# Softmax sums of the first six pairs on TensorE, and second weight pieces in earlier steps

## The chip, the cores and the metric

The kernel runs on one core of a Trainium2 chip. The metric is the time of one execution in microseconds of device time. The engines of the core each work through a queue of their own, in order: TensorE (PE, matrix products), VectorE (DVE), ScalarE (ACT), GpSimd (POOL) and SyncE (SP, which here only issues DMAs). They wait for one another by semaphores.

## The reference

Attention with soft-capped scores, and behind it a channel-mix block (batch 8, 12 heads, 448 positions, head size 64, model width 768, inner width 1024), all in 32-bit floats:

```
scores = cap * tanh(q @ k.T / sqrt(64) / cap)
attn = exp(scores - max(scores))
attn = attn / (sum(attn) + 1e-9)
x = attn @ v                       # heads side by side: (8, 448, 768)
xk = mu_k * x + (1 - mu_k) * x_prev   # x_prev: x one position earlier
xr = mu_r * x + (1 - mu_r) * x_prev
out = sigmoid(xr @ w_r) * (relu(xk @ w_k) ** 2 @ w_v)
```

The weights come as 64-bit floats, which the kernel reads as pairs of 32-bit words and turns into 32-bit floats on the chip.

## The kernel before, in words

Two heads make a pair, and there are 48 pairs. A table of operations, `STEP`, is written out once per step i (0 to 54), and the order of its words is the order of each engine's queue. In one step the stages of different pairs stand side by side: scores, tanh, exp and the reductions of pair i; the value products and the reciprocals of pair i-1; normalizing and mixing of pair i-2; loading of pair i+3. No scheduler changes that order.

Scores are computed transposed, keys on the partitions and 448 queries along the row, in four groups S0 to S3 (three of 128 keys for both heads, one with the last 64 keys of both). Each group is three products, since q and k are split into a high and a low part (`qk_high`, `qk_low`, on POOL: names qkh and qkl). PSUM holds two groups at a time, so S2 waits for the first tanh of its step and S3 for the second, S0 of the next step for the third and S1 of the next step for the fourth. ACT runs tanh and exp on each group (names p). PE's order in a step is S0, S1, the value products V of the pair before (name pv; in even steps also the "tails", the products of the last 64 keys of two pairs), S2, and S3.

The softmax sum runs over keys, that is over partitions. Before, DVE adds within 32x32 blocks while it transposes them (`red`, line 240), four DMAs gather the partial sums into 32 partitions (`gather`), DVE adds these and forms the reciprocal (`recip`), one DMA stores it to DRAM and two load it back, spread over 64 partitions each (`rec_store`, `rec_load`). `norm` (line 265) multiplies the value product by it. Then ACT scales the shifted row (`mix_old`, between the third tanh and the third exp in ACT's queue), DVE adds the other part (`mix_new`, name xk, line 280) and POOL splits it into xkh and xkl.

From step 7 on PE also multiplies the mixed x by w_k in every step, in four portions of six products (`K`, name kps, two PSUM banks in `ps_k`), and ACT applies relu and stores the result.

Alongside, the weights are converted in 44 pieces of 384 columns. One piece is loaded in each step; `more` loads a second one in some steps, before in steps 6 to 10. At a step's end ACT takes the absolute value of a loaded piece; in the next step DVE runs five instructions on the first piece ("f", lines 412 to 420: wt, wa, wa, wt, wsq), which stand ahead of the reductions, and if there is a second piece, five more in `weight_rest`, behind the third reduction. POOL adds the two parts (`weight_sum`) and, for w_k, writes the high part wkh; DVE subtracts the low part at the start of the next step (`weight_low`, name wkl). In POOL's queue weight_sum stands ahead of qk_high and qk_low of the step, then come xkh and xkl, then weight_sum of a second piece.

After the 48 pairs comes a second stage with the products by w_v and w_r, which the change does not touch.

Of the kernel before, what the change touches and what calls it, by code (L numbers as in the profile page):

```python
# [10 lines left out]
F32 = mybir.dt.float32  # L11
F32R = mybir.dt.float32r
AF = mybir.ActivationFunctionType
ALU = mybir.AluOpType
# [3 lines left out]
B, H, S, D = 8, 12, 448, 64  # L18
# [11 lines left out]
P = 128  # L30
# [12 lines left out]
HALF = (slice(0, 64), slice(64, 128))  # L43
NB = 2 * S // 32
P1, P2, P3, P4, P5, P6, P7 = range(7)
LATE = 12


# [3 lines left out]

STEP = """gather load_v weight_load more weight_low S0 S1 V S2 f f f f f tanh0 exp0 red0
weight_sum tanh1 exp1 red1 norm recip rec_store K qk_high qk_low tanh2 relu mix_old k_store mix_new x_high x_low gate_old
K exp2 red2 weight_rest weight_sum relu k_store S3 K K tanh3 exp3 red3 gate_new relu k_store weight_abs load_qk rec_load tail_open x_store weight_store"""


def f(ap):
# [3 lines left out]
class Body:  # L62
# [61 lines left out]
    def init_sums(self, pool):  # L124


        nc = self.nc
        self.r1, self.sq, self.sr = [], [], []
        for j in range(2):
            self.r1.append(pool.tile([P, NB, 4], F32, name=f"r1_{j}"))  # L130
            nc.gpsimd.memset(self.r1[j], 0.0)
            for h in range(2):
                p = slice(64 - 64 * ((h + j) % 2), 96 - 64 * ((h + j) % 2))
                nc.vector.tensor_copy(self.r1[j][p, h * NB // 2:(h + 1) * NB // 2, 3], self.grd[p].to_broadcast([32, NB // 2]))
            self.sq.append(pool.tile([32, 4, NB, 4], F32, name=f"sq_{j}"))
            self.sr.append(pool.tile([32, 32], F32, name=f"sr_{j}"))
            nc.gpsimd.memset(self.sr[j], 1.0)

    def init_attn(self):
        self.raw, self.QK, self.rawv, self.S, self.P32, self.PV, self.R, self.rs = ({} for _ in range(8))  # L140
        self.tails = []


# [72 lines left out]
    def values(self, i):  # L216

        nc, v = self.nc, self.rawv.pop(i)
        self.PV[i] = pv = self.ps_v.tile([P, 512], F32, name="pv")
        for g in range(3):  # L220
            ph = self.P32.pop((i, g))
            for h, p in enumerate(HALF):
                nc.tensor.matmul(pv[p, 0:S], v[:, g, h, :], ph[:, h, :], start=(g == 0), stop=False)  # L223
        self.tails.append((i, v))
        if i % 2:

            for j, v in self.tails:
                ph = self.P32.pop((j, 3))
                for h, p in enumerate(HALF):
                    t = HALF[(h + j) % 2]  # L230
                    nc.tensor.matmul(self.PV[j][p, 0:S], v[t, 3, h, :], ph[t, 0, :], start=False, stop=True)  # L231
            self.tails = []

    def red(self, i, g):
        r1, p32 = self.r1[i % 2], self.P32[i, g]
        for p, h, out in [(slice(0, P), slice(0, 2), r1[:, :, g])] if g < 3 else \
                [(HALF[(h + i) % 2], slice(0, 1), r1[HALF[(h + i) % 2], h * NB // 2:(h + 1) * NB // 2, 3]) for h in range(2)]:
            self.nc.vector.tensor_reduce(out=out, in_=p32[p, h].rearrange("p h (b k) -> p (h b) k", k=32),  # L240
                                         axis=mybir.AxisListType.X, op=ALU.add, apply_transpose=True)

    def gather(self, i):
        for q in range(4):
            self.nc.sync.dma_start(self.sq[i % 2][:, q], self.r1[i % 2][32 * q:32 * q + 32])

    def recip(self, i):
        nc, t = self.nc, self.sr[i % 2]
        nc.vector.tensor_reduce(out=t[:, 0:NB], in_=self.sq[i % 2].rearrange("l q x g -> l x q g"),
                                axis=mybir.AxisListType.XY, op=ALU.add)  # L250
        nc.vector.reciprocal(t[:, 0:NB], t[:, 0:NB])
        self.rs[i] = self.up.tile([32, 32], F32, name="rs")
        nc.vector.transpose(out=self.rs[i], in_=t)

    def rec_store(self, i):
        self.nc.sync.dma_start(self.rec_d[i].rearrange("h (b k) -> (h b) k", k=32), self.rs.pop(i)[0:NB])

    def rec_load(self, i):
        r = self.up.tile([P, S], F32, name="r", bufs=1)
        for h in range(2):  # L260
            self.nc.sync.dma_start(r[HALF[h]], self.rec_d[i][h:h + 1, :].to_broadcast([64, S]))
        self.R[i] = r
# [374 lines left out]
    def step(self, i, KS):  # L637
# [2 lines left out]
        if self.maxima and i < NPAIR:  # L640
            self.row_maxima(i)
        pair = dict(load_qk=i + 3, qk_high=i + 2, qk_low=i + 2, load_v=i, S=i, tanh=i, exp=i, red=i)
        pair.update(dict.fromkeys("V gather recip rec_store rec_load".split(), i - 1))
        pair.update(dict.fromkeys("norm mix_old mix_new x_high x_low gate_old gate_new x_store".split(), i - 2))
        for op in STEP.split():
            j = pair.get(op)
# [10 lines left out]
            elif op == "tail_open":  # L657
                self.tail_open(i)
            elif op == "f":
                if i <= NPAIR:  # L660
                    self.fill()
            elif op == "more":
                if i in (6, 7, 8, 9, 10):
                    self.weight_load()
            else:
                getattr(self, op)()
# [170 lines left out]
```

## Time and profile before

| | us |
|---|---|
| median of 3 runs (951.23 to 955.11) | 951.86 |
| the profiled execution | 953.09 |
| its span, first to last instruction | 951.3 |
| PE busy | 898.3 |
| DVE busy | 749.8 |
| ACT busy | 633.3 |
| POOL busy | 400.0 |

The rows are read in microseconds from the span's start. A busy time is what an engine spent on its instructions; the bracket at a row's end is the idle time just ahead of it on that engine, with the instruction that ended it. Matmuls are pipelined: two that follow one another overlap in their rows, so a stretch of them is measured from the start of the first to the start of what comes next.

### The profile page before, as it was taken

The page shows a single profiled execution, that of the slowest core. Times are in us where ns is not written, and L with a number is a line of the kernel's source. Part 1 is how long each engine was busy: PE and PEld are TensorE (multiplying, and loading weights), DVE is VectorE, ACT ScalarE, POOL GpSimd, SP SyncE. Part 2 cuts the span into 40 slices and gives each one's busy share as a digit, 9 for nine tenths or more (in the row PEclk, how much of TensorE's full clock was granted, in tenths as well). Part 3 has the DMA queues.
Part 4 walks back from the last instruction along what each step waited for, and adds up shares of the span by engine and source line. Part 5 has one row for each costly group of instructions (what it writes and reads, how often), then busy time and mean ns, then how long its engine had stood idle before and what let it go on. Part 6 is the DMA issues. An engine that isn't in the chain of part 4 may idle for free.

```text
span 951.3 us, 15131 instructions
## 1 busy us (share of the span) xinstructions
PE 898.3 (94%) x4986; PEld 720.0 (76%) x4986; DVE 749.8 (79%) x1284; ACT 633.3 (67%) x941; POOL 400.0 (42%) x350
## 2 busy tenths in 40 slices
PE   6779979999999999999999966999999999999996
PEld 3336546776677666776667865999999999999996
DVE  7999998888888888888677364887777866777775
ACT  6877777888888878878777254556556544555553
POOL 4575566666677666776652300000000013434430
PEclk8889989999999999999999979999999999999999
DMA  4555555666666656565443535544444436766763
GB/s 150 165 177 191 171 164 182 215 198 195 212 198 199 210 191 223 180 195 190 160 137 109 189 127 172 179 152 154 161 162 163 148 107 195 226 214 210 220 218 112
DMA packets 122007, 169.45 MB, mean 178 GB/s; under 512 B 22464, under 2 KB 106048, under 8 KB 121920
## 3 DMA queue, kind: packets, MB, share of 16 engines
q1 hardware_dynamic: 112704, 153.72, 50.8%
q10 hardware_dynamic: 9216, 14.68, 4.1%
q8 instruction: 41, 0.67, 0.3%
q14 instruction: 46, 0.38, 0.1%
HBM read 109.45 MB, written 56.14 MB: 174 GB/s over the span
## 4 chain that ended last, share of the span: by engine, by line
PE 78%; DVE 9%; ACT 5%; DMA 3%; issue 3%; SPq 1%; POOL 0%; ACTq 0%; DVEq 0%; POOLq 0%
PE ps L543 36%; PE kps L353 19%; PE s L196 11%; PE pv L223 10%; DVE r L240 3%; ACT p L214 2%; PE pv L231 2%; ACT p L204 2%; DMA src<-k_d 1%; DVE wa L414 1%; DVE wa L416 1%; DVE wvl L467 1%; DVE x L265 1%; DMA k_d<-ko 1%; DMA sq<-r 1%
## 5 line engine op out<-in xcount | busy, mean ns | idle before, releaser
L240 DVE TRANSPOSE_TENSOR_REDUCE r<-p 128x28 f32<-128x896 f32 (+1 forms) x240 | 217.5, 917 | 26.9 <-ACT p L214 22.9
L204 ACT ACTIVATE p<-s,scl_t 128x896 f32<-128x896 f32 x192 | 173.2, 902 | 37.8 <-PE s L196 29.9
L214 ACT ACTIVATE p<-p,cap_t 128x896 f32<-128x896 f32 x192 | 181.9, 947 | 4.8
L353 PE MATMUL kps<-xkh,wkh 128*128 128x448 f32 x372 | 141.2, 380 | 7.4 <-ACT ko L360 7.4
L543 PE MATMUL ps<-wvh,hi 128*128 128x384 f32 x392 | 132.1, 337 | 9.1 <-ACT hi L527 7.8
L353 PE MATMUL kps<-xkh,wkl 128*128 128x448 f32 x372 | 136.5, 367 | 0.0
L353 PE MATMUL kps<-xkl,wkh 128*128 128x448 f32 x372 | 136.3, 366 | 0.0
L543 PE MATMUL ps<-wvl,hi 128*128 128x384 f32 x392 | 131.6, 336 | 0.0
L223 PE MATMUL pv<-p,rv 128*64 128x448 f32 x576 | 129.8, 590 | 0.0
L507 POOL TENSOR_TENSOR s<-src 128x384 f32<-128x384 f32 x14 | 14.3, 1023 | 274.4 <-DVE lo L528 274.4
L527 ACT CAST hi<-s 128x512 fp32r<-128x512 f32 (+1 forms) x112 | 63.5, 567 | 95.5 <-PE ps L543 67.4
L528 DVE TENSOR_TENSOR lo<-s,hi 128x512 fp32r<-128x512 f32 (+1 forms) x112 | 70.1, 626 | 61.7 <-ACT hi L527 46.8
L196 PE MATMUL s<-qkh 64*128 64x448 f32 (+1 forms) x336 | 84.1, 441 | 28.1 <-ACT p L204 23.2
L86 POOL TENSOR_TENSOR qkl<-rqk,qkh 128x960 fp32r<-128x960 f32 x47 | 106.8, 2273 | 3.9
L196 PEld LDWEIGHTS s<-qkh 64*128 64x128 f32 (+1 forms) x336 | 36.9, 188 | 85.2 <-ACT p L204 34.8
L427 POOL TENSOR_TENSOR wsq<-wa,wsq 128x384 f32<-128x384 f32 x44 | 44.5, 1012 | 133.7 <-DVE wsq L420 133.7
L543 PE MATMUL ps<-wrh,hi 128*128 128x384 f32 x294 | 98.9, 336 | 0.3 <-DVE o L566 0.3
L543 PE MATMUL ps<-wrl,hi 128*128 128x384 f32 x294 | 98.8, 336 | 0.0
L353 PEld LDWEIGHTS kps<-xkh,wkh 128*128 128x128 f32 x372 | 70.5, 190 | 26.1 <-issue 12.9
L223 PEld LDWEIGHTS pv<-p,rv 128*64 128x64 f32 x576 | 39.5, 145 | 66.1 <-issue 61.1
L527 ACT CAST hi<-src 128x512 fp32r<-128x512 f32 (+1 forms) x84 | 47.7, 568 | 60.2 <-PE ps L543 57.6
L543 PE MATMUL ps<-wvh,lo 128*128 128x384 f32 x392 | 84.5, 336 | 0.4 <-DVE lo L528 0.4
(95 smaller groups left out, 1805.2 us busy)
## 6 DMA issues: line engine op xcount, KB each, us to landing
rqk<-qk SPq DMA_DIRECT2D x47, 480.0 KB
k_d<-ko ACTq DMA_DIRECT2D x64, 224.0 KB
src<-k_d SPq DMA_DIRECT2D x56, 256.0 KB
rv<-v SPq DMA_DIRECT2D x48, 256.0 KB
r<-rec_d SPq DMA_DIRECT2D x96, 112.0 KB
v_d<-o SPq DMA_DIRECT2D x56, 192.0 KB
src<-x_d SPq DMA_DIRECT2D x42, 256.0 KB
vl<-v_d SPq DMA_DIRECT2D x56, 192.0 KB
```

The lines of the kernel that those rows point to most:

```text
L86: {"p": self.nc.gpsimd, "v": self.nc.vector}[e].tensor_sub(*a)
L196: nc.tensor.matmul(s[:, h, 0:S], qk[a][p, k], qk[b][p, 0:S], start=(n == 0), stop=(n == 2))
L204: self.nc.scalar.activation(p32, self.S.pop((i, g))[:, :n, 0:S], AF.Tanh, scale=self.scl_t)
L214: self.nc.scalar.activation(p32, p32, AF.Exp, scale=1.0 if self.maxima else self.cap_t)
L223: nc.tensor.matmul(pv[p, 0:S], v[:, g, h, :], ph[:, h, :], start=(g == 0), stop=False)
L231: nc.tensor.matmul(self.PV[j][p, 0:S], v[t, 3, h, :], ph[t, 0, :], start=False, stop=True)
L240: self.nc.vector.tensor_reduce(out=out, in_=p32[p, h].rearrange("p h (b k) -> p (h b) k", k=32), axis=mybir.AxisListType.X, op=ALU.add, ap ...
L353: nc.tensor.matmul(self.kps[fc][:, 0:S], w, m[:, dc, :], start=first, stop=last)
L427: {"p": self.nc.gpsimd, "v": self.nc.vector}[e].tensor_add(sq, f(a), sq)
L527: self.nc.scalar.copy(hi, x)
L528: self.nc.vector.tensor_sub(lo, x, f(hi))
L543: self.nc.tensor.matmul(o, a[:, c, :], w[:, c, :], start=first and k == 0, stop=last and k == len(todo) - 1, skip_group_check=True)
```

## The change

For pairs 0 to 5 (`EARLY = 6`) the reductions, the gather, the reciprocal of the gathered sums, its store and its loads are left out. In their place `values` calls `sums`: eight products of the same exponentials by a tile of ones, of 64 columns, written to 64 partitions per head, so that each partition of a head's half holds the sum over all keys; for the group with the last keys a tile with ones on one half of the partitions picks the head. They are written to a bank of `ps_k`, which is free in these steps. At the step's end `recip_early` transposes the sums from PSUM in 32x32 blocks, adds the guard value to one column of each block and takes its reciprocal, copies it over the 32 columns, and transposes back; the result r has the layout that `rec_load` gave. Second weight pieces are loaded in steps 1 to 5 instead of 6 to 10.

```diff
+EARLY = 6
...
-K exp2 red2 weight_rest weight_sum relu k_store S3 K K tanh3 exp3 red3 gate_new relu k_store weight_abs load_qk rec_load tail_open x_store weight_store"""
+K exp2 red2 weight_rest weight_sum relu k_store S3 K K tanh3 exp3 red3 gate_new recip_early relu k_store weight_abs load_qk rec_load tail_open x_store weight_store"""
...
+        self.ones = self.up.tile([P, 3, D], F32, name="ones", bufs=1)
+        nc.gpsimd.memset(self.ones, 0.0)
+        nc.gpsimd.memset(self.ones[:, 0, :], 1.0)
+        for t in range(2):
+            nc.gpsimd.memset(self.ones[HALF[t], 1 + t, :], 1.0)
...
         self.tails.append((i, v))
+        if i < EARLY:
+            self.sums(i, heads)
         if i % 2:
...
+    def sums(self, i, p32):
+
+        nc, ones = self.nc, self.ones
+        self.SM[i] = ps = self.ps_k.tile([P, 512], F32, name="kps")
+        for g in range(4):
+            for h, p in enumerate(HALF):
+                w, x = (ones[:, 0, :], p32[g][:, h, :]) if g < 3 else (ones[:, 1 + (h + i) % 2, :], self.P32[i, 3][:, 0, :])
+                nc.tensor.matmul(ps[p, 0:S], w, x, start=(g == 0), stop=(g == 3))
+
+    def recip_early(self, i):
+        if not 0 <= i < EARLY:
+            return
+        nc = self.nc
+        t = self.up.tile([P, S], F32, name="sm", bufs=1)
+        c = self.up.tile([P, S // 32, 1], F32, name="sc", bufs=1)
+        nc.vector.transpose(out=t, in_=self.SM.pop(i)[:, 0:S])
+        nc.vector.tensor_scalar(c, t.rearrange("p (b k) -> p b k", k=32)[:, :, 0:1], self.grd, None, op0=ALU.add)
+        nc.vector.reciprocal(c, c)
+        nc.vector.tensor_copy(t.rearrange("p (b k) -> p b k", k=32), c.to_broadcast([P, S // 32, 32]))
+        self.R[i] = r = self.up.tile([P, S], F32, name="r", bufs=1)
+        nc.vector.transpose(out=r, in_=t)
+
     def red(self, i, g):
+        if i < EARLY:
+            return
...
     def gather(self, i):
+        if i < EARLY:
+            return
...
     def recip(self, i):
+        if i < EARLY:
+            return
...
-        pair.update(dict.fromkeys("V gather recip rec_store rec_load".split(), i - 1))
+        pair.update(dict.fromkeys("V gather recip rec_store rec_load recip_early".split(), i - 1))
...
             elif op == "more":
-                if i in (6, 7, 8, 9, 10):
+                if i in (1, 2, 3, 4, 5):
                     self.weight_load()
```

`rec_store` and `rec_load` begin with the same two lines as `red`.

PE's queue in step 2 before, from the value products of pair 1 to S2 (pv are the value products, line 231 the tails, s the scores; x2 are the two heads):

```order
L223 MATMUL pv<-p_2_309,rv 64x448 x2
L223 MATMUL pv<-p_2_315,rv 64x448 x2
L223 MATMUL pv<-p_2_328,rv 64x448 x2
L231 MATMUL pv<-p_1_257,rv 64x448 x2
L231 MATMUL pv<-p_1_336,rv 64x448 x2
L196 MATMUL s<-qkh 128x448 x2
L196 MATMUL s<-qkh,qkl 128x448 x2
```

and with the change (all lines of the file below the new functions have other numbers):

```order
L231 MATMUL pv<-p_2_316,rv 64x448 x2
L231 MATMUL pv<-p_2_321,rv 64x448 x2
L231 MATMUL pv<-p_2_328,rv 64x448 x2
L253 MATMUL kps<-p_2_316,ones 64x448 x2
L253 MATMUL kps<-p_2_321,ones 64x448 x2
L253 MATMUL kps<-p_2_328,ones 64x448 x2
L253 MATMUL kps<-p_1_335,ones 64x448 x2
L241 MATMUL pv<-p_1_259,rv 64x448 x2
L241 MATMUL pv<-p_1_335,rv 64x448 x2
L202 MATMUL s<-qkh 128x448 x2
L202 MATMUL s<-qkh,qkl 128x448 x2
```

The eight products by ones stand between the value products and the tails, ahead of S2.

DVE's queue in step 5 before, from wkl to the reciprocal of the gathered sums (wt, wa and wsq are a weight piece, line 240 the reductions, x is norm, xk is mix_new):

```order
L440 TENSOR_TENSOR wkl<-wsq,wkh 128x3x128
L412 TENSOR_SCALAR wt<-wsq 128x384
L414 TENSOR_SCALAR wa<-wt 128x384
L416 SCALAR_TENSOR_TENSOR wa<-w_540,wa 128x384
L418 TENSOR_SCALAR wt<-wa 128x384
L420 SCALAR_TENSOR_TENSOR wsq<-w_540,wt 128x384
L240 TENSOR_REDUCE r_1_197<-p_2_672 128x28
L240 TENSOR_REDUCE r_1_197<-p_2_678 128x28
L265 TENSOR_TENSOR x_160<-pv,r 128x448
L249 TENSOR_REDUCE sr_195<-sq_194 32x28
L251 RECIPROCAL sr_195<-sr_195 32x28
L253 STREAM_TRANSPOSE rs<-sr_195 32x32
```

and in step 4 with the change, from norm to the last transposition (kps are the sums, sm and sc the transposed ones and their column, r the reciprocals):

```order
L307 TENSOR_TENSOR x_158<-pv,r 128x448
L322 SCALAR_TENSOR_TENSOR xk<-x_158,mu_k,pv 128x448
L454 TENSOR_SCALAR wt<-wsq 128x384
L456 TENSOR_SCALAR wa<-wt 128x384
L458 SCALAR_TENSOR_TENSOR wa<-w_465,wa 128x384
L460 TENSOR_SCALAR wt<-wa 128x384
L462 SCALAR_TENSOR_TENSOR wsq<-w_465,wt 128x384
L261 STREAM_TRANSPOSE sm<-kps 128x448
L262 TENSOR_SCALAR sc<-sm,grd 128x14
L263 RECIPROCAL sc<-sc 128x14
L264 COPY sm<-sc 128x448
L266 STREAM_TRANSPOSE r<-sm 128x448
```

Behind norm and xk there now stand a second weight piece and the five instructions of recip_early; the reductions, the reduction of the gathered sums, its reciprocal and the small transposition are gone.

DVE's queue in step 6 with the change, from the last instruction of the first piece to the half reductions, which recip_early follows:

```order
L462 SCALAR_TENSOR_TENSOR wsq<-w_675,wt 128x384
L274 TENSOR_REDUCE r_0_195<-p_2_831 128x28
L274 TENSOR_REDUCE r_0_195<-p_2_837 128x28
L307 TENSOR_TENSOR x_158<-pv,r 128x448
L322 SCALAR_TENSOR_TENSOR xk<-x_158,mu_k,pv 128x448
L274 TENSOR_REDUCE r_0_195<-p_2_846 128x28
L454 TENSOR_SCALAR wt<-wsq 128x384
L456 TENSOR_SCALAR wa<-wt 128x384
L458 SCALAR_TENSOR_TENSOR wa<-w_677,wa 128x384
L460 TENSOR_SCALAR wt<-wa 128x384
L462 SCALAR_TENSOR_TENSOR wsq<-w_677,wt 128x384
L274 TENSOR_REDUCE r_0_195<-p_1_868 64x14 x2
```

Step 6 holds the old reductions (pair 6), a second piece and recip_early (pair 5) together; before, its reductions stood with one piece and no recip_early.

## Rows read from the trace of the kernel before

**Rows 1.** The page's parts 1 and 2: busy time of each engine with its share of the span and its instructions, and the TensorE clock that was granted, in tenths of full speed, in 40 equal slices of the span.

```profile
PE 898.3 (94%) x4986; PEld 720.0 (76%) x4986; DVE 749.8 (79%) x1284; ACT 633.3 (67%) x941; POOL 400.0 (42%) x350
...
PEclk8889989999999999999999979999999999999999
```

**Rows 2.** Busy time of each engine by stretches: the stretch (us from the span's start) and its length, then busy us of PE, PEld, DVE, ACT and POOL with the count of instructions, the granted clock, the share of the DMA engines and GB/s. The three stretches are steps 1 to 6, steps 7 to 12, and from step 13 on.

```profile
13.81:72.47 58.66, 46.07 (x222) 19.57 (x222) 53.52 (x94) 47.81 (x60) 35.48 (x34) 0.83 0.52 160
72.47:150.75 78.28, 69.83 (x366) 45.36 (x368) 74.46 (x129) 55.71 (x74) 48.08 (x46) 0.93 0.53 172
150.75:500.00 349.25, 349.25 (x1984) 240.24 (x1981) 293.74 (x489) 285.80 (x362) 233.73 (x189) 1.00 0.60 193
```

**Rows 3.** The timeline of PE: the first products of S1 (second score group of a pair) in steps 2, 7, 14 and 16. Columns: start us, us, engine, line, operation, output and inputs, shapes, count, and in brackets the idle time ahead and what ended it.

```profile
23.34 0.47 PE L196 MATMUL s<-qkh 64*128 64x448 f32 x2 [0.63 <-ACT p L204]
...
72.47 0.48 PE L196 MATMUL s<-qkh 64*128 64x448 f32 x2 [1.04 <-ACT p L204]
...
161.09 0.38 PE L196 MATMUL s<-qkh 64*128 64x448 f32 x2
...
182.65 0.38 PE L196 MATMUL s<-qkh 64*128 64x448 f32 x2
```

**Rows 4.** The timeline of PE, steps 1, 5 and 6, same columns: S2 of step 1; then S1, the value products and S2 of step 5; then S1, the value products, the tails and S2 of step 6.

```profile
19.76 0.47 PE L196 MATMUL s<-qkh 64*128 64x448 f32 x2
...
52.10 0.47 PE L196 MATMUL s<-qkh 64*128 64x448 f32 x2 [1.04 <-ACT p L204]
...
52.90 2.48 PE L223 MATMUL pv<-p,rv 128*64 128x448 f32 x12
55.31 0.47 PE L196 MATMUL s<-qkh 64*128 64x448 f32 x2
...
61.67 0.74 PE L196 MATMUL s<-qkh 64*128 64x448 f32 x2 [2.62 <-ACT p L204]
...
63.08 4.57 PE L223 MATMUL pv<-p,rv 128*64 128x448 f32 x12
67.58 0.98 PE L231 MATMUL pv<-p,rv 64*64 64x448 f32 x8
68.50 0.47 PE L196 MATMUL s<-qkh 64*128 64x448 f32 x2
```

**Rows 5.** The timeline of ACT, same columns: the third tanh of step 1; mix_old of step 5; then the third tanh, mix_old, third exp and last tanh of step 6.

```profile
20.69 1.01 ACT L204 ACTIVATE p<-s,scl_t 128x896 f32<-128x896 f32 x1 [1.83 <-DVE sr L249]
...
59.49 0.64 ACT L275 ACTIVATE pv<-x,om_k 128x448 f32<-128x448 f32 x1 [1.46 <-DVE x L265]
...
69.40 1.01 ACT L204 ACTIVATE p<-s,scl_t 128x896 f32<-128x896 f32 x1 [2.70 <-PE s L196]
70.31 0.63 ACT L275 ACTIVATE pv<-x,om_k 128x448 f32<-128x448 f32 x1
70.87 1.03 ACT L214 ACTIVATE p<-p,cap_t 128x896 f32<-128x896 f32 x1
71.80 0.62 ACT L204 ACTIVATE p<-s,scl_t 128x448 f32<-128x448 f32 x1
```

**Rows 6.** The timeline of DVE, same columns, step 5: wkl, the first and second instruction of a weight piece, the first two reductions behind it, and norm; then xk of step 6.

```profile
54.13 0.56 DVE L440 TENSOR_TENSOR wkl<-wsq,wkh 128x384 fp32r<-128x384 f32 x1
54.60 0.35 DVE L412 TENSOR_SCALAR wt<-wsq 128x384 f32<-128x384 f32 x1
54.99 0.36 DVE L414 TENSOR_SCALAR wa<-wt 128x384 uint32<-128x384 uint32 x1
...
56.85 2.10 DVE L240 TRANSPOSE_TENSOR_REDUCE r<-p 128x28 f32<-128x896 f32 x2
58.87 0.59 DVE L265 TENSOR_TENSOR x<-pv,r 128x448 f32<-128x448 f32 x1
...
71.05 0.68 DVE L280 SCALAR_TENSOR_TENSOR xk<-x,mu_k,pv 128x448 f32<-128x448 f32 x1 [0.72 <-ACT pv L275]
```

**Rows 7.** The timeline of DVE, same columns, step 7: first, second and last instruction of the second weight piece.

```profile
82.54 0.53 DVE L412 TENSOR_SCALAR wt<-wsq 128x384 f32<-128x384 f32 x1
83.10 1.19 DVE L414 TENSOR_SCALAR wa<-wt 128x384 uint32<-128x384 uint32 x1
...
85.32 0.56 DVE L420 SCALAR_TENSOR_TENSOR wsq<-w,wt 128x384 f32<-128x384 uint32 x1
```

**Rows 8.** The timeline of POOL, same columns: qkl and xkl of step 7, then weight_sum and qkl of step 8.

```profile
80.05 2.27 POOL L86 TENSOR_TENSOR qkl<-rqk,qkh 128x960 fp32r<-128x960 f32 x1
...
82.94 1.15 POOL L86 TENSOR_TENSOR xkl<-xk,xkh 128x448 fp32r<-128x448 f32 x1
...
90.95 1.02 POOL L427 TENSOR_TENSOR wsq<-wa,wsq 128x384 f32<-128x384 f32 x1 [2.92 <-DVE wsq L420]
...
93.62 2.23 POOL L86 TENSOR_TENSOR qkl<-rqk,qkh 128x960 fp32r<-128x960 f32 x1
```

**Rows 9.** The view of one source line, the four copies of the guard value at the start: line, engine, operation, output and input, count: shortest, median and longest duration in ns, first and last start in us, shapes.

```profile
L134 DVE COPY r<-grd x4: 163/521/2174, 7.5 to 9.9; 32x14 f32<-32x14 f32 x4
```

**Rows 10.** Groups of instructions by line and shape over the whole span: line, engine, operation, output and inputs, shapes, count | busy us, mean ns of one | idle time ahead and what ended it.

```profile
L240 DVE TRANSPOSE_TENSOR_REDUCE r<-p 64x14 f32<-64x448 f32 x96 | 61.5, 640 | 12.9 <-ACT p L214 9.6
...
L251 DVE RECIPROCAL sr<-sr 32x28 f32<-32x28 f32 x48 | 15.2, 316 | 1.7
...
L253 DVE STREAM_TRANSPOSE rs<-sr 32x32 f32<-32x32 f32 x48 | 9.6, 199 | 1.6
```

More of the change, by code (lines that the diff above doesn't have):

```diff
@@ L139, in init_attn @@
     def init_attn(self):
-        self.raw, self.QK, self.rawv, self.S, self.P32, self.PV, self.R, self.rs = ({} for _ in range(8))
+        self.raw, self.QK, self.rawv, self.S, self.P32, self.PV, self.R, self.rs, self.SM = ({} for _ in range(9))
         self.tails = []
@@ L219, in values @@
         self.PV[i] = pv = self.ps_v.tile([P, 512], F32, name="pv")
+        heads = []
         for g in range(3):
             ph = self.P32.pop((i, g))
+            heads.append(ph)
             for h, p in enumerate(HALF):
@@ L255, in rec_store @@
     def rec_store(self, i):
+        if i < EARLY:
+            return
         self.nc.sync.dma_start(self.rec_d[i].rearrange("h (b k) -> (h b) k", k=32), self.rs.pop(i)[0:NB])
     def rec_load(self, i):
+        if i < EARLY:
+            return
         r = self.up.tile([P, S], F32, name="r", bufs=1)
```

## The prediction

> **What bounds the kernel now.** I read the page's totals first. TensorE (PE) is busy for 94% of the span and nothing else comes near; its clock row falls below 9 tenths only in slices 1, 2, 3, 6 and 25 of forty [rows 1]. The stretches then say where PE waits [rows 2]. From 150.75 to 500 us PE never stops and runs at full clock, so whatever is late at 150 us is late at the end, one for one. Before 150.75 it does wait: 46.07 busy of 58.66 us in steps 1 to 6, 69.83 of 78.28 in steps 7 to 12, at granted clocks of 0.83 and 0.93. There VectorE (DVE) is the fullest engine, 53.52 and 74.46 us.
>
> I measure a step from one start of its second score product ("S1") to the next [rows 3]. S1 of step 2 starts at 23.34, of step 7 at 72.47: 9.83 us a step. From there to step 14 (161.09) it is 88.62 us, 12.66 a step, though two settled steps take 21.56 (161.09 to 182.65), 10.78 each. Steps 7 to 11 are those with a second weight piece. At most 88.62 - 75.46 = 13.2 us can be won there, and the change also lays new work on the steps ahead of them.
>
> **Term 1: the sums on PE.** Each of six pairs gets eight fp32 products (sixteen instructions), in the same column halves as the value products, of which twelve instructions take 2.41 us (52.90 to 55.31) [rows 4]. Sixteen take 3.21. They stand between the value products and S2, in PE's only queue, and nothing hides them, because S2 starts the chain that closes the step: S1 to values 0.80, values 2.41, S2 to its tanh 0.90 (68.50 to 69.40), tanh to mix_old 0.91, mix_old to exp 0.56, exp to the last tanh 0.93, and that to the next S1 0.67 (71.80 to 72.47) [rows 4, 5]. That is 7.18 us, or 8.10 with the 0.92 of the tails in even steps. With the sums it is 10.39 and 11.31. Before, the step took longer than this chain because DVE held it; now 10.85 on average is a floor above the old 9.83. Step 1 simply gets 3.21 more, since its third tanh had stood idle for 1.83 us and started at 20.69, 0.93 behind the S2 of 19.76: S1 of step 2 comes at 26.55.
>
> **Term 2: DVE in steps 2 to 5.** Out go the reductions of a pair, 2 x 1.05 + 1.05 + 1.3 = 4.45 us (two take 2.02, 56.85 to 58.87; a half one 0.64), and the gathered reciprocal, 1.1 (a small reduction as long as norm, 0.32 and 0.20) [rows 6, 10]. In come a second weight piece with its wkl, and the new chain of five. No row has a transposition of 128x448: the 32x32 one takes 0.20 and fourteen of these would be 2.8; the reduction that transposes 448 columns takes 0.64, and I take that, being of the same width, with 0.4 to 2.8 as bounds. The add (0.2), the reciprocal of 14 columns (0.2, below the 0.32 of 28) and the copy (0.4, by the 0.36 of a tensor_scalar of 384) are small: 2.1 us a chain, 1.6 to 6.4 at the ends [rows 10].
>
> Taken quietly, the work from one norm to the next is: norm to mix_old 0.62 and mix_old to xk 0.74, xk 0.68, together 2.0; second piece 2.25 (54.60 to 56.85); chain 2.1; two wkl 0.95; first piece 2.25 [rows 5, 6]. The sum of 9.55 would lie under PE's 10.85. But it is not quiet. A DVE copy lasted 2174 ns of a median of 521 at 7.5 to 9.9 us, where GpSimd (POOL) ran its first splits [rows 9], and in step 7 the second instruction of a second piece lasted 1.19 instead of 0.36: it started at 83.10 and ended 0.2 after POOL's xkl (82.94 to 84.09) [rows 6 to 8]. So a DVE tensor_scalar or copy waits out the POOL instruction that it meets. In before the first pieces met an idle POOL, since POOL was itself waiting for their result; second pieces came behind red2. Now the order puts the second piece directly behind xk. POOL, released by the first piece, ends qkl 4.9 us after starting weight_sum (90.95 to 95.85) [rows 8], which is about when norm starts; xk ends 2.0 after that. So wt stands for 2.9 us, and then shares the port with xkh and xkl: in step 7 the piece ended 3.6 us after qkl's end (82.32 to 85.88) [rows 7, 8], the quiet price would be 2.25, and I take 2.7 since a waiting instruction goes first. Piece: 5.6 (5.2 to 6.5). Behind it the chain's add meets weight_sum of that very piece, 0.5 more: chain 2.6. Norm to norm is then 2.0 + 5.6 + 2.6 + 0.95 + 2.25 = 13.4, and DVE holds the step again: norm waits behind it, ACT's mix_old for norm, exp and tanh behind mix_old, S1 behind tanh, and xkh on POOL for xk.
>
> The Trainium skill ("SBUF — State Buffer", Who interferes with whom) says of this that DVE and GpSimd take turns on one port pair for whole instructions, and it lets a DVE instruction with two SBUF inputs wait as well. No row here shows the latter. By it the fourth and fifth instructions of a piece could stand too; at half a microsecond a piece I estimate 2 us more in all.
>
> **Term 3: the seam.** Step 6 has everything: pair 6 is reduced in the old way, its second piece and the sixth chain come too. Ahead of its norm stand 2.1 us of reductions: 15.5. From there to norm in step 7: 2.0, red2 1.05, piece 3.4 (as in step 7, 82.54 to 85.88, qkl being over), the half reductions 1.3, chain 2.6, wkl and piece 3.2, reductions 2.1: 15.65.
>
> **Term 4: steps 8 to 13** lose the second piece. DVE then has some 9.7 us a step, PE 10.78, so PE sets them and its waits there go: 6 x 10.78 = 64.7.
>
> **Sum.** S1 of step 2 at 26.55; step 2 11.3; step 3 11.3 (xk of step 2 ends 10.6 after S1 by PE's chain, piece 3.4 and chain 2.6 carry DVE 5.3 into step 3, wkl and piece 3.2 bring norm to 8.5, and 2.8 follow to the next S1); steps 4 and 5 26.8; step 6 15.5; step 7 15.65; steps 8 to 13 64.7. S1 of step 14 comes at 171.8 instead of 161.09: 10.7 us late. The profiled execution took 953.09, 1.2 above the median of 951.86: 963.8 beside the profile, 962.6 beside the median. The queue of SyncE loses 42 transfers (gather, store, loads), and the second weight load of a step waits there for its buffer, some 5 us into the step, with load_qk behind it; both are wanted only near the step's end or in the next, so I cost this at nothing. The memsets of ones stand ahead of a POOL that waits for its first data, and cost nothing either.
>
> **Rivals.**
> *POOL hardly holds DVE.* Then steps 2 to 5 run on PE's floor (43.4), step 6 takes 11.65, step 7 14.0 (the same lists with 2.25 and 2.1), the rest 64.7: S1 of step 14 at 160.3, -0.8 us, and with a dearer chain up to +3: 951 to 955. For it: the pieces' place may shift by a microsecond or two and miss qkl. Against: the 1.19 of rows 7, and POOL follows DVE, so the meeting repeats.
> *The clock falls.* In steps of 13.4 PE has about 9.2 of work, idle 4.3. Behind an idle of 2.62 us the values at 63.08 took 4.57, until 67.58 [rows 4]. If values and sums both ran so (4.5 + 6.0), the chain would be near 16.5 and steps 4 to 6 some 7 us longer: 966 to 971. Against: by the S2 of 68.50 the clock was back, so it would hit the values and little of the sums.
> *Transpositions by blocks.* At 2.8 each the chain is 6.4, 4.3 more in five steps: 980 and above.
> *Faster.* A single mechanism would be that the sums are cheap: column halves and their unchanging ones at half the price, 1.6 us. Then PE's floor is 9.25, DVE's quiet 9.55 sets the steps at the old pace, step 7 on is PE's: 942 to 946. It decides where sums cost under 2 us and POOL does not hold DVE; no row says either. Even with full price and every DVE delay hidden it is 26.55 + 54.7 + 75.5 = 156.75, -4.3 us.
>
> **Numbers.** About 0.5%, 4.8 us, is what a measurement can tell here: faster is below 947.1, slower above 956.6. Forecast 0.55, quiet POOL 0.20, clock 0.16, dear transposition 0.05, faster 0.04. The forecast's own range is 957 to 966. The range goes from 952, within the quiet case, to 973, above the clock's. Slower: 0.55 + 0.16 + 0.05, and no part of quiet, 0.76; same 0.20; faster 0.04.
>
> **What would show it.** Sums: sixteen instructions of kps at 0.2 us behind each of six value groups, and S2's tanh idle for PE about 3 us. Port: wt or wa of second pieces over 1.5 us in steps 3 to 5, ending with POOL's qkl or xkl. Chain: two transpositions near 0.64. Seam: steps 6 and 7 over 15 us. Steps 8 to 13 near 10.8 with PE never idle. I am wrong if steps 3 to 5 take under 11.5 us, or PE still waits after step 8.

## The result and the profile after

| | before | after |
|---|---|---|
| median, us | 951.55 (4 runs) | 963.9 (4 runs: 962.22 to 966.38) |
| ratio, 95% interval | | 1.0124 [1.009, 1.0157] |
| the profiled execution | 953.09 | 962.22 |
| its span | 951.3 | 960.4 |
| S1 of step 7 | 72.47 | 90.33 |
| S1 of step 14 | 161.09 | 171.85 |

The changed kernel is slower by 1.2%, 12.4 us in the medians. The page of the changed kernel, part 1 [rows 1 for before]:

```profile
PE 916.2 (95%) x5082; PEld 727.1 (76%) x5082; DVE 739.3 (77%) x1266; ACT 632.8 (66%) x941; POOL 399.9 (42%) x354
```

PE has 96 more instructions (six pairs of sixteen) and is busy 17.9 us longer; DVE is busy 10.5 us less. Neither number is the loss. Where it lies is told by the stretches, here steps 2 and 3, 4 and 5, 6 and 7, and 8 to 13 (columns as in [rows 2], each stretch from an S1 to an S1):

```profile
25.45:47.58 22.13, 18.44 (x106) 8.02 (x106) 14.22 (x27) 17.04 (x23) 10.47 (x12) 1.00 0.30 96
47.58:74.76 27.18, 21.85 (x106) 8.87 (x106) 24.94 (x39) 17.12 (x23) 16.39 (x17) 0.87 0.40 134
74.76:105.56 30.80, 24.84 (x115) 12.66 (x116) 28.84 (x49) 16.70 (x22) 18.08 (x17) 0.83 0.20 63
105.56:171.85 66.29, 66.29 (x366) 44.93 (x368) 56.45 (x98) 54.15 (x70) 39.67 (x37) 0.97 0.58 188
```

In the first stretch neither PE (18.44) nor DVE (14.22) fills the 22.13 us: a chain through several engines sets them. In the second DVE is at 24.94 of 27.18, in the third at 28.84 of 30.80: there it is DVE. In the fourth PE never stops. Before, S1 of step 8 to S1 of step 14 took 78.25 us (82.84, in the timeline of PE, to 161.09 [rows 3]); now it is 66.29. That gain of 12 us is real; the seven steps ahead of it lost 22.7.

```profile
82.84 0.38 PE L196 MATMUL s<-qkh 64*128 64x448 f32 x2
```

The timeline of PE, the S1 of steps 2, 4, 6 to 9 and 14, with the value products, sums and tails of step 4 (columns as in [rows 3]):

```profile
25.45 0.47 PE L202 MATMUL s<-qkh 64*128 64x448 f32 x2 [0.63 <-ACT p L210]
...
47.58 0.47 PE L202 MATMUL s<-qkh 64*128 64x448 f32 x2 [1.87 <-ACT p L210]
...
48.39 4.17 PE L231 MATMUL pv<-p,rv 128*64 128x448 f32 x12
52.39 3.18 PE L253 MATMUL kps<-p,ones 128*64 128x448 f32 x16
55.49 0.98 PE L241 MATMUL pv<-p,rv 64*64 64x448 f32 x8
...
74.76 0.47 PE L202 MATMUL s<-qkh 64*128 64x448 f32 x2 [2.73 <-ACT p L210]
...
90.33 0.74 PE L202 MATMUL s<-qkh 64*128 64x448 f32 x2 [3.80 <-ACT p L210]
...
105.56 0.47 PE L202 MATMUL s<-qkh 64*128 64x448 f32 x2 [1.77 <-ACT p L210]
...
118.56 0.37 PE L202 MATMUL s<-qkh 64*128 64x448 f32 x2
...
171.85 0.36 PE L202 MATMUL s<-qkh 64*128 64x448 f32 x2
```

Steps 2 to 8 take 11.1, 11.0, 13.6, 13.6, 15.6, 15.2 and 13.0 us, where before it was 9.4 to 10.8 in steps 2 to 7 and 13.7 in step 8. The sums take 3.10 us (52.39 to 55.49).

The timeline of DVE around this: norm, xk, the five instructions of the second piece, first and last of the new chain of five, the two wkl, and the next norm ([rows 6, 7] show the same instructions before):

```profile
44.76 0.62 DVE L307 TENSOR_TENSOR x<-pv,r 128x448 f32<-128x448 f32 x1
46.08 0.68 DVE L322 SCALAR_TENSOR_TENSOR xk<-x,mu_k,pv 128x448 f32<-128x448 f32 x1 [0.71 <-ACT pv L317]
46.68 1.03 DVE L454 TENSOR_SCALAR wt<-wsq 128x384 f32<-128x384 f32 x1
47.74 2.30 DVE L456 TENSOR_SCALAR wa<-wt 128x384 uint32<-128x384 uint32 x1
50.07 0.79 DVE L458 SCALAR_TENSOR_TENSOR wa<-w,wa 128x384 uint32<-128x384 uint32 x1
50.90 1.18 DVE L460 TENSOR_SCALAR wt<-wa 128x384 uint32<-128x384 uint32 x1
52.11 0.56 DVE L462 SCALAR_TENSOR_TENSOR wsq<-w,wt 128x384 f32<-128x384 uint32 x1
52.59 0.64 DVE L261 STREAM_TRANSPOSE sm<-kps 128x448 f32<-128x448 f32 x1
...
54.63 0.65 DVE L266 STREAM_TRANSPOSE r<-sm 128x448 f32<-128x448 f32 x1
55.20 0.98 DVE L482 TENSOR_TENSOR wkl<-wsq,wkh 128x384 fp32r<-128x384 f32 x2
...
58.35 0.62 DVE L307 TENSOR_TENSOR x<-pv,r 128x448 f32<-128x448 f32 x1
```

and of POOL beside it (columns the same):

```profile
46.50 0.99 POOL L77 TENSOR_SCALAR qkh<-rqk 128x960 fp32r<-128x960 f32 x1
47.58 2.25 POOL L87 TENSOR_TENSOR qkl<-rqk,qkh 128x960 fp32r<-128x960 f32 x1
49.78 0.68 POOL L77 TENSOR_SCALAR xkh<-xk 128x448 fp32r<-128x448 f32 x1
50.55 1.31 POOL L87 TENSOR_TENSOR xkl<-xk,xkh 128x448 fp32r<-128x448 f32 x1
```

Lay them side by side: wt ends 0.2 us after qkh, wa 0.2 after qkl, the second wt 0.2 after xkl. A quiet piece takes 2.25 [rows 6]; this one takes 5.9 (46.68 to 52.59). Norm to norm is 13.6, which is the step.

### The profile page after: what moved, and what is told of

It is laid out like the page before. It is cut to its first block, busy times and chain, and to the rows that moved or that the text cites. A ratio compares the mean times of both kernels' runs of the same rounds, so it can differ in the third digit from the quotient of the medians.

```text
span 960.4 us, 15238 instructions
## 1 busy us (share of the span) xinstructions
PE 916.2 (95%) x5082; PEld 727.1 (76%) x5082; DVE 739.3 (77%) x1266; ACT 632.8 (66%) x941; POOL 399.9 (42%) x354
## 4 chain that ended last, share of the span: by engine, by line
PE 62%; DVE 11%; POOL 7%; DMA 5%; ACT 5%; issue 4%; SPq 4%; ACTq 0%; DVEq 0%; POOLq 0%
PE ps L585 36%; PE kps L395 11%; PE s L202 7%; PE pv L231 7%; DMA sq<-r 3%; SPq L281 3%; POOL xg L340 2%; POOL xkl L87 2%; ACT p L220 2%; ACT p L210 1%; PE pv L241 1%; DVE xg L334 1%; DMA src<-k_d 1%; DVE r L274 1%; POOL qkl L87 1%
## 5 line engine op out<-in xcount | busy, mean ns | idle before, releaser
L274 DVE TRANSPOSE_TENSOR_REDUCE r<-p 128x28 f32<-128x896 f32 (+1 forms) x210 | 190.6, 917 | 36.5 <-ACT p L220 33.6
```

## The experiments

S1 of step 14 is the best yardstick: from there to the end of the span all kernels but e7 and e8 take 788.6 to 794.4 us. It comes from one profiled execution of each kernel; how much it varies between executions was not measured. The ratio is against the kernel before, run beside each.

| kernel | S1 of step 7 | S1 of step 14 | median | ratio [95%] |
|---|---|---|---|---|
| before | 72.47 | 161.09 | | |
| changed | 90.33 | 171.85 | 963.90 | 1.0124 [1.0090, 1.0157] |
| e1 sums alone | 81.13 | 170.82 | 964.08 | 1.0104 [1.0072, 1.0136] |
| e2 pieces alone | 85.89 | 163.65 | 956.06 | 1.0024 [1.0009, 1.0039] |
| e3 piece elsewhere | 89.06 | 169.98 | 963.28 | 1.0096 [1.0062, 1.0129] |
| e4 e3, sums behind S2 | 84.66 | 165.33 | 959.32 | 1.0067 [1.0043, 1.0091] |
| e5 changed, no qkl on POOL | 86.49 | 167.40 | 961.30 | 1.0092 [1.0056, 1.0128] |
| e6 e1, sums behind S2 | 71.56 | 161.08 | 955.53 | 1.0016 [0.9995, 1.0037] |
| e7 before, norm first | 71.39 | 158.52 | 1019.05 | 1.0658 [1.0597, 1.0720] |
| e8 e7, pieces spread | 79.43 | 160.98 | 1020.66 | 1.0713 [1.0675, 1.0752] |
| e9 e7, recip back | 71.30 | 159.94 | 954.38 | 1.0011 [0.9991, 1.0031] |
| e10 e5, sums behind S2 | 82.41 | 161.71 | 955.49 | 1.0027 [1.0009, 1.0044] |
| e11 two pieces past the seam | 88.22 | 169.93 | 961.93 | 1.0081 [1.0054, 1.0108] |
| e12 mixed | 79.19 | 156.00 | 951.53 | 0.9967 [0.9951, 0.9984] |

### Each half by itself: e1 and e2

e1 takes the pieces back; e2 takes the sums back (`EARLY = 0`).

```diff
-                if i in (1, 2, 3, 4, 5):
+                if i in (6, 7, 8, 9, 10):
```

> The products with ones and the reciprocals from PSUM stay, the second weight pieces go back to steps 6 to 10. Theory (sums lengthen PE's chain in every step, and the second pieces only move the loss about): steps 2 to 5 fall to PE's floor of 10.4 and 11.3 us, the steps with second pieces go back to 13 to 14, S1 of step 14 comes at 171 to 172, time 960 to 964, about that of the changed kernel. Rival (the early pieces and their meeting with POOL are the whole cause): without them the time falls back to 949 to 954.

Steps 2 to 6 took 11.1, 10.2, 11.1, 11.9 and 11.1 us (in the fifth the value products took 4.0 us, 58.91 to 62.92, at a granted clock of 0.57); 8.7 us of the 9.7 lost stand in steps 1 to 6. S1 of step 14 and the time lie 0.2 and 0.1 us outside their bounds, on opposite sides; the rival fell. The busy times of e1 in steps 2 to 6, and from the timeline of DVE the xk just ahead of S1 of step 6:

```profile
25.68:81.13 55.45, 48.29 (x270) 20.57 (x270) 32.10 (x62) 40.04 (x51) 30.94 (x30) 0.97 0.36 112
```

```profile
68.60 0.68 DVE L322 SCALAR_TENSOR_TENSOR xk<-x,mu_k,pv 128x448 f32<-128x448 f32 x1 [5.18 <-ACT pv L317]
```

DVE is busy for 32.10 of 55.45 us and waits 5.18 us for mix_old: it holds nothing. The sums alone cost almost the whole loss, and DVE's saving buys nothing, because DVE was not the one waited for once PE's chain is longer.

> The second pieces come in steps 1 to 5, the sums are reduced on DVE and gathered as before. Theory: steps 2 to 5 are set by DVE (two pieces and reductions, the second piece held by POOL's qkl), 13 to 15 us each, steps 8 to 13 run on PE near 10.8, S1 of step 14 comes at 164 to 167, time 954 to 959. Rival (the sums on PE are the whole cause): the early pieces are a gain by themselves, time 940 to 950. Second rival (the pieces are the whole cause): 962 to 966 as in the changed kernel.

Step 2 took 9.4 us, not the 13 to 15 of the theory, as its second piece shows only in step 3; steps 3 to 7 took 13.3 to 13.5 us, steps 9 to 13 10.3 to 11.2: the pieces by themselves cost 13.4 us up to S1 of step 7 and win 10.9 behind it. The time is in the theory's bounds, S1 of step 14 0.35 us ahead of them. So neither half is the whole cause, and they don't add (9.7 and 2.6 alone, 10.8 together): that fits two limits over the same steps, of which the later one counts, and e4, e5 and e10 test it. In e2 a reduction stands between xk and the second piece, and the meeting with POOL is cheaper. The second piece's first two instructions in e2:

```profile
46.14 0.46 DVE L454 TENSOR_SCALAR wt<-wsq 128x384 f32<-128x384 f32 x1
46.63 1.19 DVE L456 TENSOR_SCALAR wa<-wt 128x384 uint32<-128x384 uint32 x1
```

These two stand 0.9 us over the quiet price; in the changed kernel four instructions of the piece stand 3.7 over it.

### The place of the sums: e6

```diff
-... S0 S1 V S2 f f f f f tanh0 ...
+... S0 S1 V S2 sums f f f f f tanh0 ...
```

In e6 (and e4, e10, e12) `values` keeps the tiles and `sums` is a word of its own.

> The kernel with the sums alone (second pieces in steps 6 to 10), the products with ones behind the third score product group (S2) instead of ahead of it. Theory (what the sums cost in steps 2 to 6 is their place in the chain, not their 3.2 us of PE's time): steps 2 to 6 fall from 11.1 to 8.7 to 9.8 us, S1 of step 7 comes at 71 to 75 instead of 81.13, S1 of step 14 at 161 to 165, time 952 to 957. Rival (the amount of PE's work sets the steps): steps stay near 11, time 962 to 965.

Steps 2 to 6 took 9.7, 8.8, 9.7, 8.8 and 10.0, the last 0.2 above the bounds. The timeline of PE in step 3 of e6 (columns as in [rows 4]):

```profile
38.39 3.23 PE L254 MATMUL kps<-p,ones 128*64 128x448 f32 x16
41.55 0.47 PE L202 MATMUL s<-qkh 128*128 128x448 f32 x1
...
43.15 0.47 PE L202 MATMUL s<-qkh 64*128 64x448 f32 x2
```

The same sixteen instructions last 3.16 us, S1 of the next step no longer waits, and S1 of step 14 is where it was before (161.08 against 161.09). So the 9.7 us of e1 are the price of the place, ahead of S2 and so inside the chain, not of PE's time.

### The meeting with POOL: e3 and e5

e3 moves the second piece and its weight_sum, with the same work on every engine:

```diff
-... norm recip rec_store K qk_high qk_low tanh2 ... exp2 red2 weight_rest weight_sum relu ...
+... norm recip rec_store K weight_rest weight_sum qk_high qk_low tanh2 ... exp2 red2 relu ...
```

> The changed kernel with the second piece moved in the order of a step: from behind red2, where POOL's qk_high and qk_low run, to ahead of qk_high and qk_low on both engines. The amount of work on every engine is the same. Theory (the collision on the port costs some 3.5 us a piece in steps 3 to 5): wt and wa of the second piece take their quiet 0.3 to 0.5 us, steps 3 to 5 take 11 to 12 us instead of 13.6, S1 of step 14 comes at 163 to 165, time 953 to 957. Rival (the amount of DVE's work sets the steps, the place is indifferent): the time stays at 962 to 966.

The theory's number was missed: only 1.9 us came back. The reason is in the timeline of DVE in e3, around the chain of step 3:

```profile
38.00 0.24 DVE L263 RECIPROCAL sc<-sc 128x14 f32<-128x14 f32 x1
38.28 0.86 DVE L264 COPY sm<-sc 128x448 f32<-128x448 f32 x1
39.17 0.65 DVE L266 STREAM_TRANSPOSE r<-sm 128x448 f32<-128x448 f32 x1
39.74 2.72 DVE L482 TENSOR_TENSOR wkl<-wsq,wkh 128x384 fp32r<-128x384 f32 x2
```

and of POOL:

```profile
37.90 0.99 POOL L77 TENSOR_SCALAR qkh<-rqk 128x960 fp32r<-128x960 f32 x1
38.98 2.25 POOL L87 TENSOR_TENSOR qkl<-rqk,qkh 128x960 fp32r<-128x960 f32 x1
```

The second piece is quieter (2.9 us by its rows, 0.86, 0.56, 0.56, 0.36 and 0.56), but now the copy waits for qkh, the two wkl take 2.72 instead of 0.98 beside qkl, and the next wt (1.29 at 42.39) ends 0.2 us after xkl. Norm to norm fell from 13.6 to 12.9. DVE had no gap, and the waits for POOL's splits passed to the instructions that now stood beside them. This fits the rival in its number, not in its mechanism, and e5 tells them apart, since it leaves DVE's list as it is and takes qkl from POOL (the subtraction is left out, and ACT copies in its place, 0.98 us a step; the scores are other numbers, the instructions of PE and DVE the same):

```diff
-        self.sub(e, lo, self.raw.pop(i), f(hi))
+        self.copy("a", lo, self.raw.pop(i))
```

> The changed kernel, but qk_low leaves out its subtraction: ACT copies the raw tile into the low part instead, so POOL no longer runs qkl (2.25 us a step), and the score products that use the low part are other numbers. DVE's list of instructions is the same. Theory (DVE waits out POOL's splits on a shared port): wa of the second piece no longer takes 2.30 us in steps 3 to 5, the piece falls from 5.9 to 3 to 4 us, steps 4 and 5 from 13.6 to 11.3 to 12.3 us, S1 of step 14 comes at 165 to 168 instead of 171.85, time 956 to 960. Rival (the amount of DVE's own work sets the steps): the piece keeps 5 us or more, the time 962 to 966.

The piece fell to 4.0 us (48.10 to 52.08 in step 4), steps 4 and 5 to 12.8 and 11.0, and S1 of step 14 to 167.40, 4.5 us earlier; the median, 961.3, came out 1.3 above the range, step 4 half a microsecond above its own and step 5 0.3 below. The first instruction of the piece of step 4, and of the chain behind it:

```profile
48.10 1.02 DVE L454 TENSOR_SCALAR wt<-wsq 128x384 f32<-128x384 f32 x1
...
52.08 0.64 DVE L261 STREAM_TRANSPOSE sm<-kps 128x448 f32<-128x448 f32 x1
```

With DVE's own work unchanged, that is the price of qkl. What still waits there waits for qkh (wt at 48.10, 1.02) or for xkl; the third instruction of the second piece on DVE and xkl on POOL, e5, step 5:

```profile
61.94 1.40 DVE L458 SCALAR_TENSOR_TENSOR wa<-w,wa 128x384 uint32<-128x384 uint32 x1
```

```profile
61.77 1.16 POOL L87 TENSOR_TENSOR xkl<-xk,xkh 128x448 fp32r<-128x448 f32 x1
```

Step 5 of e5 at 11.0 is still DVE's. Step 4 is PE's: the 11.1 us of an even step in e1, and 1.7 more because its value products took 4.17 us instead of 2.48; DVE's xk waits 1.76 us for mix_old there, of which mix_old itself is 0.7. So behind DVE's limit PE's stood at once.

### Both limits gone: e4 and e10

> As the run before, and the products with ones stand behind the third score product group (S2) in PE's queue instead of ahead of it. Theory (sums ahead of S2 lengthen the chain S1 to values to S2 to tanh by 3.2 us; behind S2 they run while ACT works): the steps 2 to 7 shorten by about 0.7 us each against the run before, S1 of step 14 comes at 159 to 161, time 948 to 952. Rival (PE's amount of work, not its place, costs): as the run before, 953 to 957.

Steps 1 to 3 fell to 9.9, 9.7 and 9.9, but steps 4 and 5 stayed at 12.9, DVE's norm to norm with the collisions of e3. The theory's 948 to 952 was missed for the reason that e3 shows; against e3 the sums' place is worth 4.65 us at S1 of step 14. The changed kernel with the sums behind S2 and nothing else was not run.

> The changed kernel with both suspected costs gone at once: the products with ones behind S2, and qk_low left out as in the run e5_low_on_act (ACT copies the raw tile into the low part, so the score products that use it are other numbers). Theory (the place of the sums and the meeting with qkl are two separate limits, PE's and DVE's, of the same steps): steps 1 to 3 at 9.5 to 10.8 us, steps 4 and 5 at 10.5 to 11.5, S1 of step 14 at 161 to 165, so within 4 us of before, and what is left stands in steps 6 and 7. Rival (one limit alone): as the better of e4_order_behind (165.33) and e5_low_on_act (167.4), or later.

S1 of step 14 is at 161.71: of the 10.8 us lost, 10.1 are back. That is ahead of both e4 (165.33) and e5 (167.40), so one limit alone does not explain the loss. Steps 1 to 8 took 9.9, 9.7, 10.7, 11.7, 11.7, 13.6, 14.7 and 11.3 (steps 4 and 5 are 0.2 above their bounds), so that what early pieces still cost is in steps 3 to 7, and it is as large as what steps 8 to 13 win.

### The seam: e11

```diff
-                if i in (1, 2, 3, 4, 5):
+                if i in (1, 2, 3, 7, 8):
```

> The changed kernel with two of its five second pieces moved from steps 4 and 5 to 7 and 8 (steps 1, 2, 3, 7, 8). Theory (the steps from S1 to S1 that took 13.6, 15.6 and 15.2 us are DVE's: early piece, reductions of pair 6 and sixth chain together): the fifth step falls to PE's 11 or 12 us, the sixth and seventh fall to 12 to 13, the ninth and tenth grow to 12.5 to 14, S1 of step 14 at 167 to 171, time 958 to 963. Rival (steps 6 and 7 are long for another reason, the change of the way the sums are made): they stay at 15 and the time rises to 966 or more.

Steps 6 and 7 fell from 15.6 and 15.2 to 12.8 and 11.8, steps 10 and 11 rose to 13.5 and 12.1. Step 5 stayed at 13.6, against 11 or 12 expected: a piece loaded in step 3 is converted in step 4 and still delays the S1 that ends step 5, so the moved pieces show one step later than put. So the seam is the second piece beside the reductions of pair 6 and the chain, and moving these two pieces carried most of the cost to where they went: S1 of step 14 came 1.9 us earlier.

### Other ways to win: e7, e8, e9 and e12

e7 is the kernel before with norm ahead of two reductions:

```diff
-... tanh0 exp0 red0
-weight_sum tanh1 exp1 red1 norm recip rec_store ...
+... tanh0 exp0
+weight_sum tanh1 exp1 norm recip red0 red1 rec_store ...
```

> The kernel before, with one thing moved on DVE: norm and the small reciprocal stand ahead of the reductions of the first two groups (red0, red1) instead of behind them. Theory (where DVE holds a step, it is because norm, and behind it mix_old, exp, tanh and S1, stand behind 2.1 us of reductions that nothing waits for): S1 of step 7 comes 1 to 3 us earlier than 72.47, S1 of step 14 at 156 to 160 instead of 161.09, time 947 to 951. Rival (DVE's amount of work sets the steps, its order is indifferent): time as before, 951 to 955.

> As the run before, and the second weight pieces in steps 2, 4, 6, 8 and 10 instead of 6 to 10, so that no two follow each other. Theory (a second piece costs a step some 4 us wherever DVE is full, and some 2.5 where PE's 10.8 already covers a part): steps with early pieces grow to 13 to 14, the later ones without fall to 10.4 to 11.3, and the sum is the same within 2 us, S1 of step 14 at 156 to 160, time 947 to 952. Rival (the backlog of pieces in a row is what costs): 2 to 4 us less than the run before.

The early part did what was said in e7 (158.52 at S1 of step 14); in e8 it is 160.98, a microsecond past the bounds. As a whole they are 66 and 68 us slower. The waits of DVE over the whole span of e7, and its busy times from 161 to 500 us, where PE never stopped before [rows 2]:

```profile
DVE sr L287 <- DMA sq<-r: 94.3, 42, 4.8
```

```profile
161.00:500.00 339.00, 299.02 (x1631) 200.09 (x1628) 243.97 (x423) 236.35 (x303) 195.08 (x159) 0.97 0.53 170
```

The small reciprocal, moved with norm ahead of 2.1 us of reductions, now comes before the gathered sums have landed, and all of DVE stands behind it, 42 times, where before it waited 13.2 us in all. e9 puts it back (`norm red0 red1 recip`):

> The kernel before, with the order norm, red0, red1, recip on DVE instead of red0, red1, norm, recip: norm goes first, as in the run e7_norm_first, but the small reciprocal keeps its time, so that it no longer meets the gather transfer that it waited for. Theory (in e7_norm_first the early steps won 2.6 us, 158.52 instead of 161.09, and the loss came from recip waiting 94 us in all for the gathered sums): S1 of step 14 comes at 157 to 160, recip never waits, time 947 to 951. Rival (norm first also delays the sums, their way through memory and so the next norm, wherever recip stands): time 960 and above.

S1 of step 14 at 159.94 is in the bounds; the time is that of before, and the 947 to 951 us of the theory were missed. "Recip never waits" was wrong: it waits 16.7 us in 14 times. But this is nothing new, as the group of the same reduction in the kernel before shows (columns as in [rows 10]). New is that norm, put 2.1 us earlier, waits for the loads of the reciprocals, 18 times in e9 and once, for 0.7 us, before:

```profile
L249 DVE TENSOR_REDUCE sr<-sq 32x28 f32<-32x448 f32 x48 | 28.6, 595 | 13.5 <-DMA sq<-r 13.2
```

```profile
DVE x L307 <- DMA r<-rec_d: 12.8, 18, 1.4
```

What takes back the 1.2 us won by step 14 is not shown.

e12 uses all of it (norm first with recip behind the reductions, sums behind S2, second piece directly behind the first, pieces in steps 1, 2, 4, 8 and 10), and qk_high on ACT:

```diff
-        self.copy(e, hi, self.raw[i])
+        self.copy("a" if 2 <= i < 14 else e, hi, self.raw[i])
```

> Every finding put together in one kernel that computes the reference: products with ones behind S2 for pairs 0 to 5; second pieces in steps 1, 2, 4, 8 and 10, so that not two early steps in a row are full; the second piece directly behind the first on DVE, where POOL has not started its splits; norm ahead of the reductions and the small reciprocal behind them; qk_high on ACT in pairs 2 to 13, so that POOL is done with its splits 1 us sooner. Theory (with PE's chain and the meetings with POOL out of the way, early pieces are cheap): steps 1 to 5 at 9 to 11 us, S1 of step 14 at 154 to 159 instead of 161.09, time 945 to 951. Rival (the meetings with POOL only move, as in the run e3_order, and what is won in later steps is paid in the early ones): S1 of step 14 at 160 to 165, time 952 to 957.

It is faster than before by 0.33%, 2.2 us in the medians, and so the best of all kernels here, though only S1 of step 14 (156.00) lies within the theory's bounds; the median is 0.5 above them, and steps 3 and 4 took 12.3 and 12.1 instead of 9 to 11. Of the 5.1 us won there, about 3 are given back behind it. Busy times of e12 from S1 of step 14 on, and what PE waited for until 530 us:

```profile
156.00:500.00 344.00, 340.95 (x1932) 233.81 (x1929) 281.48 (x477) 274.78 (x353) 228.07 (x184) 1.00 0.61 191
```

```profile
PE pv L231 <- DVE xk L323: 2.3, 5, 0.8
```

Before, PE waited for nothing in these steps; here it is idle for 3.05 us up to 500 us. Norm stands first in all steps, and from 156 to 530 us it waits 10.7 us in 12 times for the loads of the reciprocals; that this is what holds xk back is argued, as norm first in steps 1 to 13 alone was not tried.

## Why the prediction was right

The forecast was 962.6; measured were 963.9 and, in the profiled execution, 962.22 against 963.8 in the prediction's sum. By its steps:

**Term 1, sums on PE.** Right. 3.10 us against 3.21 (28.56 to 31.66 and 52.39 to 55.49), and steps 2 and 3 at 11.1 and 11.0 against 11.3. e1 shows the floor alone, 11.1 us on average against 10.85, and e6 shows that it is a matter of the place: "nothing hides them, because S2 starts the chain" was the right reason. Step 1 was mis-sized: S1 of step 2 came at 25.45, not 26.55, because the value products of step 1 took 3.79 us and not 4.60; that the clock came back sooner there is argued from these durations alone.

**Term 2, DVE in steps 4 and 5.** Right in size: 13.6 against 13.4. The piece took 5.9 against 5.6 (bounds 5.2 to 6.5), the chain 2.6 against 2.6, with transpositions at 0.64 and 0.65 against the 0.64 taken. The prediction's own sign of being wrong, "if steps 3 to 5 take under 11.5 us", was drawn too wide: step 3 took 11.0, as its sum had put it at 11.3. The way there was a little other than put: not wt stood for 2.9 us, but wt for qkh, wa for qkl and the second wt for xkl, each in turn. e5 shows that qkl is the main cause, with 1.9 of the 3.7 us; what the prediction did not see is that another place for the piece would not cure it (e3).

The Trainium skill's rule ("SBUF — State Buffer", Who interferes with whom), that a DVE instruction with two inputs in SBUF waits for POOL as well, was held open in the prediction, which named the fourth and fifth instruction of a piece; the two with such inputs are the third and the fifth (L458 and L462). The runs agree: L458 with two such inputs took 1.40 beside xkl (e5) instead of 0.56, and the two wkl of e3 took 2.72 instead of 0.98. In the changed kernel it cost L458 0.84 us once (1.40 at 36.69) and 0.23 in each of the next three pieces, where POOL was just ending xkh, and L462 nothing: 1.5 us in all against the 2 that the prediction estimated.

**Term 3, the seam.** Right: 15.6 and 15.2 against 15.5 and 15.65. mix_old waited for norm there, as the timeline of ACT shows for steps 6 and 7 (1.46 in [rows 5] before):

```profile
88.16 0.64 ACT L317 ACTIVATE pv<-x,om_k 128x448 f32<-128x448 f32 x1 [2.64 <-DVE x L307]
...
103.38 0.64 ACT L317 ACTIVATE pv<-x,om_k 128x448 f32<-128x448 f32 x1 [5.02 <-DVE x L307]
```

**Term 4, steps 8 to 13.** Mis-sized by 1.6 us: 66.3 against 64.7. Step 8 took 13.0, 1.8 more than the other even steps (11.2), as its value products ran at the lower clock after the long step 7 (granted clock 0.58 from 106.36 to 110.40, 1.00 behind it; PE at 106.36, in the timeline):

```profile
106.36 4.17 PE L231 MATMUL pv<-p,rv 128*64 128x448 f32 x12
```

"PE still waits after step 8" did not come about: PE has no idle time from 105.56 to 171.85. S1 of step 14 came at 171.85 against 171.8, because steps 1 to 3 were 1.6 us shorter than put and step 8 longer; that the two errors cancel is luck.

**From there to the end** the prediction carried the 10.7 us on one for one. The profiled spans differ by 9.1 and the medians by 12.4, the profiled execution of the changed kernel being the fastest of its four; the rest of a span varies by some 6 us over the kernels, and what sets it was not looked into. So a forecast within 1.3 us of the median is better than its terms could promise, and in part luck.

**The rivals.** *POOL hardly holds DVE* fell with wa at 2.30. *The clock falls* was half true: value products took 4.17 to 4.74 us in steps 4 to 8, near the double of 2.41 (granted clock 0.57 in step 4, so for the most part the lower of the two levels, 1.2 and not 2.4 GHz), but sums always ran at full clock (3.17 to 3.18; 1.00 in step 4), and in steps 4 to 7 PE's longer work lies beside DVE's. It decides only where PE's chain sets the step, as in step 8 and in step 4 of e5. *Transpositions by blocks* fell with 0.64. *Faster* by cheap sums fell with 3.10; and in e6 and e10, where the sums cost nothing, the time is still not below that of before.

## What to carry to other kernels

Work moved to an engine with idle time is free only if it stands where nothing waits for what comes next: the same 3.1 us a step cost 9.7 us over six steps ahead of S2 and nothing behind it, so look at the chain through the step, not at the busy share. Two engines that hold each other up have to be counted together: DVE had no gap here, so another order (e3) mostly carried the waits to other instructions, and less work on POOL (e5) took them away. An order that puts only instructions that are not held beside POOL's splits was not tried; e2, where a reduction stood beside them (0.9 us for the piece instead of 3.7), points that way. An instruction that waits for a transfer must not be moved ahead of the work that covered it; 2.1 us earlier cost 66.

## What the runs showed of the hardware

Not all DVE instructions wait for POOL. Beside qkh, qkl or xkl, TENSOR_SCALAR, COPY and those with two inputs in SBUF were held (0.36 became 2.30, 0.39 became 0.86, 0.56 became 1.40), while in e3 the transposition r<-sm from SBUF to SBUF took 0.65 in the middle of qkl and the reciprocal 0.24 beside qkh, as in quiet. The timeline of DVE in step 1 of the changed kernel, with POOL idle, has the same two durations and shows the copy's quiet price:

```profile
22.95 0.24 DVE L263 RECIPROCAL sc<-sc 128x14 f32<-128x14 f32 x1
23.23 0.39 DVE L264 COPY sm<-sc 128x448 f32<-128x448 f32 x1
23.66 0.65 DVE L266 STREAM_TRANSPOSE r<-sm 128x448 f32<-128x448 f32 x1
```

PE's clock did not follow the idle time ahead of S1 alone: in e10 the value products behind an idle of 1.85 us (S1 at 45.42) took 2.48 at a granted clock of 1.00, those behind 1.82 us in the changed kernel (S1 at 61.17) 4.17 at 0.57. And a transposition of 128x448 from PSUM or within SBUF took 0.64 to 0.65 us, as long as the reduction over 448 columns [rows 10], far from fourteen times the 0.20 of a 32x32 one.
